# Retention with a mixture of adapters: warm-up, mask order, adapter weights and the pacing of transfers

## The chip, the core and the metric

The kernel runs on one core of a Trainium2 chip. The metric is the device time of one execution in microseconds. A core has TensorE (PE, with its weight loads shown apart as PEld), VectorE (DVE), ScalarE (ACT), GpSimd (POOL) and SyncE (SP). In this kernel SP computes nothing: it issues nearly all transfers between HBM and SBUF, one after the other in the order of the program. Each engine runs its own instructions in order and waits on semaphores for the others.

## The reference

Inputs are q, k, v of 8 batches x 8 heads x 576 positions x 64, and the weights of a mixture of 8 adapters of rank 16. All is float32.

```python
scores = scale * np.matmul(q, k.transpose(0, 1, 3, 2))
gamma = 1.0 - 2.0 ** (-5.0 - np.arange(H))
Dmat = np.where(rel >= 0, gamma[:, None, None] ** rel[None, :, :], 0.0)   # rel = i - j
x = np.matmul(scores * Dmat[None], v)       # then (B, H, S, D) -> rows of 4608 tokens x 512
logits = x @ w_gate                          # 512 -> 8
topk = the 2 largest logits of each token;  w = softmax over these two
out = x + sum over the two experts e of  w_e * ((x @ A[e]) @ B[e])
```

## The kernel before, in words

The 576 positions are four full chunks of 128 and a rest of 64. A **unit** is one chunk of two batches (units 0 to 15: chunk 0 of the four batch pairs, then chunk 1, and so on); units 16 and 17 are the rests of four batches each. The decay is folded into k and q: each is multiplied by a power of gamma on POOL or DVE (`scale_`, L162 to L184). From unit 2 on q is loaded with neighbouring positions in pairs and scaled into an own tile (`qs`, L169).

For a unit u PE does, in short runs of small matmuls:

- T (`stage_T`, L187; lines L215 and, for paired q, L202): transposes k and q into PSUM. ACT copies them out (`evict_T`, L231), and `shift_q` (L249) copies halves of q on DVE into a second tile, x2.
- U (`stage_U`, L291): sums k times v of each half chunk of 64 positions, for the running state. `stage_A` (L327) adds them on DVE into the state SP; `put_state` (L310) copies the state of the first half beside v, on ACT; `first_state` (L318) does so for the chunk's beginning on POOL.
- S (`stage_S`, L258): scores within a half chunk. `masks` (L279) multiplies them by a triangle on DVE, four instructions for the half t and the part of the heads ho, and writes them over x2 and qT. In these tiles each half then holds masked scores on one side and q on the other.
- X (`stage_X`, L339): one product of v and the state with masked scores and q gives x. In chunk 0, where no state comes in, the first half's products stand ahead of the second half's. ACT copies x out, transposed (`evict_x`, L360).
- Z (`stage_Z`, L388): x times the adapters' A and the gate, all in one tile AW of 136 columns. `routing_1` to `routing_4` (L402 to L448) pick two experts: a copy on ACT, maxima on DVE (`choose`), sigmoids on ACT, the mask and two products on POOL.
- P (`stage_P`, L374) transposes the result, copied out by `evict_z` on ACT; B (`stage_B`, L450) transposes x back into PSUM, Y (`stage_Y`, L469) adds the adapters' B to it, ACT copies the output (`evict_o`, L483), and `store` (L520) sends it off.

Nothing schedules this: the order on each engine is that of the program's text. Rounds up to unit 4 are written out (L575 to L845); a loop (L847) then does, for t from 5 to 16, the scores and x of unit t, the logits of t-1, the output of t-2 and the transposes of t+1. `ahead(t)` (L630) issues on SP the stores that are due and the loads of unit t+4, and lets POOL scale unit t+2. `finish` (L693) does the last unit.

PSUM has eight buffers, named by tags x0, x1, s0, s1, u0, u1, o0, o1; a stage that writes a tag waits until the tag's last reader is done. k and v have six SBUF buffers each, q five, the copied x (`xT`) three. `fill` and `fill_small` (L496 to L516) are matmuls of zeros into o0 and o1, whose result nobody reads.

At the start SP issues k, q, v of units 0, 1, 2, then the adapter weights (four transfers for A, L556, one for the gate, L560), then units 3 to 5. k of a unit is one transfer of 512 KB, q and v are two of 256 KB each.

Of the kernel before, what the change touches and what calls it, by code (L numbers as in the profile page):

```python
# [18 lines left out]
def kernel(  # L19
# [43 lines left out]
    for c in range(NFULL):  # L63
# [71 lines left out]
    def load(u, w):  # L135
        if u >= NU:
            return
        c, bp = units[u]
        s0 = 128 * c
        if c == NFULL:  # L140
            for t in range(2):
                hf = slice(64 * t, 64 * t + 64)
                dst = block(u, t)[hf] if w == "v" else nt(u, w)[hf]
                nc.sync.dma_start(out=dst, in_=rows(w, 4 * bp + 2 * t, 2, s0, 64))
        elif w == "v":
            for t in range(2):
                hf = slice(64 * t, 64 * t + 64)
                nc.sync.dma_start(  # L148
                    out=block(u, t)[hf], in_=rows(w, 2 * bp, 2, s0 + 64 * t, 64)
                )  # L150
        elif w == "q" and paired(u):
            for b in range(2):
                nc.sync.dma_start(
                    out=nt(u, w)[64 * b : 64 * b + 64].rearrange("p (h e) d -> p h (e d)", e=2),
                    in_=q[2 * bp + b, :, s0 : s0 + 128, :].rearrange(
                        "h (p e) d -> p h (e d)", e=2
                    ),
                )
# [201 lines left out]
    def evict_x(u):  # L360
        st[u]["xT"] = []
        for b in range(2):
            xt = mo.tile([128, HP, 128], FP32, tag=f"xT{b}", name=f"xT{b}", bufs=3)
            px = st[u]["px"][b]
            if paired(u):
                nc.scalar.copy(  # L366
                    out=xt.rearrange("p a (t i e) -> p (a t) e i", t=2, e=2),
                    in_=px.rearrange("p a t (e i) -> p (a t) e i", e=2),
                )
            else:  # L370
                nc.scalar.copy(out=xt, in_=px.rearrange("p a t i -> p a (t i)"))
            st[u]["xT"].append(xt)
# [121 lines left out]
    def fill_small(n):  # L494
        pf = [pp.tile([128, 96], FP32, tag=f"o{r}", name=f"pf{r}") for r in range(2)]
        for _ in range(n):  # L496
            for c in range(2):
                for r in range(2):
                    sl = slice(64 * r, 64 * r + 64)
                    nc.tensor.matmul(  # L500
                        pf[r][64 * c : 64 * c + 64],
                        lhsT=zero[sl, 0:64],
                        rhs=zero[sl, 0:96],
                        start=True,
                        stop=True,
                        skip_group_check=True,
                    )

    def fill(n):
        if n == 0:  # L510
            return
        pf = pp.tile([128, 512], FP32, tag="o1", name="pf")
        for _ in range(n):
            nc.tensor.matmul(
                pf, lhsT=zero[:, 0:128], rhs=zero, start=True, stop=True, skip_group_check=True
            )  # L516

    o3 = out.rearrange("(b s) m -> b s m", s=S)
# [1 line left out]
    def store(u):  # L520
        c, bp = units[u]
        of = st.pop(u)["osb"].rearrange("p b a o d -> p b (a o d)")
        for b in range(2):
            if c < NFULL:
                nc.sync.dma_start(
                    out=o3[2 * bp + b, 128 * c : 128 * c + 128, :], in_=of[:, b]
                )
            else:
                for t in range(2):
                    (nc.gpsimd if b and u == NU - 2 else nc.sync).dma_start(  # L530
                        out=o3[4 * bp + 2 * t + b, 128 * c : 128 * c + 64, :],
                        in_=of[64 * t : 64 * t + 64, b],
                    )


    def load_batch(u, w, b):
        c, bp = units[u]
        nc.sync.dma_start(  # L538
            out=nt(u, w)[:, b * H : b * H + H], in_=rows(w, 2 * bp + b, 1, 128 * c, 128)
        )  # L540

    nc.vector.memset(zero, 0.0)
    nc.vector.memset(warm, 0.0)
# [5 lines left out]
    load(0, "v")  # L549
    for w in "kqv":  # L550
        load(1, w)
    nc.sync.dma_start(out=pack2, in_=dr_pack2.ap())
    for w in "kqv":
        load(2, w)
    for dt in range(HP):
        nc.sync.dma_start(  # L556
            out=AW[:, dt, 0:ER].rearrange("p (e r) -> p e r", e=E),
            in_=moe_A[:, 128 * dt : 128 * dt + 128, :].rearrange("e d r -> d e r"),
        )
    nc.sync.dma_start(  # L560
        out=AW[:, :, ER : ER + E],
        in_=moe_w_gate.rearrange("(t p) e -> p t e", p=128),
    )
    for u in range(3, 6):
        for w in "kqv":
            load(u, w)

    both = (nc.gpsimd, nc.vector)
    pool2 = (nc.gpsimd, nc.gpsimd)
    dve2 = (nc.vector, nc.vector)  # L570
# [10 lines left out]
    scale_(0, "q", pool2, (0,))  # L581
    scale_(0, "k", dve2, (1,))
    scale_(0, "q", dve2, (1,))
    by_t = ((0, 0), (0, 1), (1, 0), (1, 1))
# [37 lines left out]
    evict_T(2, "q")  # L622
    shift_q(2, nc.vector)
    stage_U(2)
    put_state(2, 1, st[2]["pu"][0], nc.scalar)
    stage_S(2)
    masks(2)
    scale_(3, "k", pool2)

    def ahead(t):  # L630
        for u in {4: (0,), 5: (1, 2)}.get(t, (t - 3,)):
            if t > 3 and has(u):
                store(u)
        for w in "kqv":
            load(t + 4, w)
        if has(t + 1):
            first_state(t + 1)
        if has(t + 2):
            scale_(t + 2, "k", pool2)
            if t > 2:  # L640
                scale_(t + 2, "q", pool2)

    def scores(u):
        if has(u):
            stage_S(u)
            masks(u)
# [46 lines left out]
    def finish():  # L693
# [69 lines left out]
        def output_b(b, zt):  # L763
            o = mo.tile([128, HP, 2, 64], FP32, tag=f"oe{b}", name="oe", bufs=1, align_bytes=256)
            for ho, eng in ((0, nc.scalar), (1, nc.vector)):
                nc.tensor.matmul(
                    po[b][ho], lhsT=zt, rhs=bv[:, :, ho, :],
                    start=False, stop=True, skip_group_check=True,
                )
                (eng.copy if eng is nc.scalar else eng.tensor_copy)(  # L770
                    out=o[:, :, ho, :], in_=po[b][ho]
                )
            c, qd = units[u]
            of = o.rearrange("p a o d -> p (a o d)")
            for t in range(2):
                (nc.scalar if b and t else nc.sync).dma_start(
                    out=o3[4 * qd + 2 * t + b, 128 * c : 128 * c + 64, :],
                    in_=of[64 * t : 64 * t + 64],
                )
# [13 lines left out]
        output_b(0, zt0)  # L793
        output_b(1, small_b(1))

    stage_A(2)
    logits(0)
    choose(0)
    scale_(3, "q", both)
    products(2)  # L800
    routing_3(0)
    turn(3)
    sums(3)
    put(3)
    shift_q(3, nc.vector)
    ahead(2)

    routing_4(0)
    scores(3)
    stage_A(3)  # L810
    scale_(4, "q", both)
    ahead(3)
    logits(1)
    small(0)
    choose(1)
    back(0)
    products(3)
    output(0)
    routing_3(1)
    turn(4)  # L820
    logits(2, "x0")
    choose(2)
    sums(4)
    put(4)
    routing_3(2)
    shift_q(4, nc.vector)

    routing_4(1)
    routing_4(2)
    ahead(4)  # L830
    scores(4)
    logits(3)
    small(1)
    choose(3)
    small(2, "u0")
    back(1)
    output(1)
    sums(5)
    routing_3(3)
    turn(5)  # L840
    back(2)
    put(5)
    shift_q(5, nc.vector)
    products(4)
    output(2)  # L845

    for t in range(5, NU - 1):  # L847
# [53 lines left out]
```

## Time and profile before

| | us |
|---|---|
| median of 3 timed runs | 192.85 (192.42 to 196.5) |
| profiled execution, whole | 190.79 |
| its span, first to last instruction | 188.9 |
| PE busy in the span | 167.3 (89%) |
| ACT, DVE, POOL busy | 114.1, 113.3, 108.7 |
| transfers | 38.99 MB, mean 206 GB/s |

A group's row has the line, engine and operation, what it writes and reads, shapes, the count, then busy time, mean ns of one, and the idle time before them with what ended it. A row of the timeline has start, length, engine, line, and in brackets the idle time before. A row of the waits has who waited for whom, the total, how often, and the longest. "issue" is an idle time for which the profile has no releaser. Ends of matmuls are modelled, and neighbouring runs overlap by a little.

### The profile page before, as it was taken

The page shows a single profiled execution, that of the slowest core. Times are in us where ns is not written, and L with a number is a line of the kernel's source. Part 1 is how long each engine was busy: PE and PEld are TensorE (multiplying, and loading weights), DVE is VectorE, ACT ScalarE, POOL GpSimd, SP SyncE. Part 2 cuts the span into 40 slices and gives each one's busy share as a digit, 9 for nine tenths or more (in the row PEclk, how much of TensorE's full clock was granted, in tenths as well). Part 3 has the DMA queues.
Part 4 walks back from the last instruction along what each step waited for, and adds up shares of the span by engine and source line. Part 5 has one row for each costly group of instructions (what it writes and reads, how often), then busy time and mean ns, then how long its engine had stood idle before and what let it go on. Part 6 is the DMA issues. An engine that isn't in the chain of part 4 may idle for free.

```text
span 188.9 us, 10441 instructions
## 1 busy us (share of the span) xinstructions
PE 167.3 (89%) x4675; PEld 148.9 (79%) x4675; DVE 113.3 (60%) x227; ACT 114.1 (60%) x255; POOL 108.7 (58%) x162
## 2 busy tenths in 40 slices
PE   3989598799889889898999999999997999999960
PEld 3578498588879788788999989899996988988840
DVE  1384837665296475748577787777594846555240
ACT  3437163735569484765767868494959394674650
POOL 1333321567769988493949586675969397520240
PEclk9999969999999999999999999999999999999998
DMA  7999969999999999999999999999998853112325
GB/s 157 248 221 225 227 70 232 202 224 246 224 228 235 262 252 277 252 260 247 241 257 246 266 232 250 221 278 226 271 206 243 181 169 115 50 68 111 115 56 166
DMA packets 108075, 38.99 MB, mean 206 GB/s; under 512 B 88768, under 2 KB 103488, under 8 KB 108032
## 3 DMA queue, kind: packets, MB, share of 16 engines
q1 hardware_dynamic: 107568, 37.71, 81.1%
q8 instruction: 36, 0.59, 1.4%
q0 software_dynamic: 240, 0.39, 1.0%
q10 hardware_dynamic: 224, 0.24, 0.5%
q14 instruction: 7, 0.06, 0.1%
HBM read 29.02 MB, written 9.44 MB: 204 GB/s over the span
## 4 chain that ended last, share of the span: by engine, by line
PE 59%; SPq 14%; issue 7%; DMA 6%; POOL 5%; DVE 4%; ACT 2%; POOLq 0%; ACTq 0%
PE px L350 15%; PE pz L393 12%; PE ps_s L269 8%; PE pu L300 6%; PE po L475 5%; PE po L459 4%; PE pt_k L215 4%; SPq L148 3%; SPq L556 3%; PE pt_q L202 3%; DMA k<-in_k_dram 3%; SPq L160 3%; DMA q<-in_q_dram 3%; POOL k L179 2%; SPq L538 2%
## 5 line engine op out<-in xcount | busy, mean ns | idle before, releaser
L179 POOL TENSOR_TENSOR k<-k,pack 128x512 f32<-128x512 f32 x32 | 34.9, 1109 | 17.4 <-DMA k<-in_k_dram 16.5
L350 PE MATMUL px<-x,v 128*64 128x64 f32 (+1 forms) x576 | 39.3, 226 | 2.6 <-DVE x L289 0.8
L289 DVE TENSOR_TENSOR x<-ps_s,pack 64x512 f32<-64x512 f32 (+1 forms) x38 | 25.1, 660 | 25.9 <-PE ps_s L269 25.6
L350 PE MATMUL px<-qT,v 128*64 128x64 f32 (+1 forms) x576 | 39.2, 226 | 1.3 <-DVE qT L289 1.1
L350 PEld LDWEIGHTS px<-x,v 128*64 128x64 f32 (+1 forms) x576 | 36.2, 140 | 4.4 <-ACT kT L240 1.0
L350 PEld LDWEIGHTS px<-qT,v 128*64 128x64 f32 (+1 forms) x576 | 36.1, 140 | 1.9 <-DVE qT L289 1.2
L393 PE MATMUL pz<-AW,xT 128*128 128x136 f32 x272 | 36.1, 286 | 0.6 <-ACT kT L240 0.6
L393 PEld LDWEIGHTS pz<-AW,xT 128*128 128x128 f32 x272 | 32.6, 190 | 1.8 <-ACT kT L240 0.8
L169 POOL TENSOR_TENSOR qs<-q,pack 128x512 f32<-128x512 f32 x25 | 26.1, 1062 | 4.1 <-DMA q<-in_q_dram 4.1
L406 ACT COPY zs<-pz 128x272 f32<-128x272 f32 x17 | 6.6, 386 | 33.2 <-PE pz L393 32.5
L289 DVE TENSOR_TENSOR qT<-ps_s,pack 64x512 f32<-64x512 f32 (+1 forms) x38 | 25.1, 660 | 1.1
L269 PE MATMUL ps_s<-qT,kT 64*64 64x64 f32 x1152 | 23.6, 224 | 2.1 <-issue 1.4
L269 PEld LDWEIGHTS ps_s<-qT,kT 64*64 64x64 f32 x1152 | 20.4, 137 | 6.2 <-issue 3.1
L441 POOL TENSOR_TENSOR cm<-ge,sg 128x16 f32<-128x16 f32 x17 | 4.0, 234 | 36.5 <-PE pt_k L215 16.9
L316 POOL COPY v<-SP 64x512 f32<-64x512 f32 x32 | 20.5, 640 | 1.6
L300 PE MATMUL pu<-v,k 64*64 64x64 f32 x1024 | 19.2, 221 | 0.8 <-DMA v<-in_v_dram 0.8
L240 ACT COPY kT<-pt_k 128x512 f32<-128x512 f32 x34 | 18.2, 589 | 1.2 <-PE pt_k L215 1.0
L253 DVE COPY x<-qT 64x512 f32<-64x512 f32 x17 | 14.5, 852 | 7.4 <-ACT qT L235 5.0
L366 ACT COPY xT<-px 128x512 f32<-128x512 f32 x28 | 16.3, 625 | 4.4 <-PE px L350 4.4
L300 PEld LDWEIGHTS pu<-v,k 64*64 64x64 f32 x1024 | 16.9, 134 | 2.5 <-DMA v<-in_v_dram 0.9
L492 ACT COPY osb<-po 128x512 f32<-128x512 f32 x33 | 17.6, 584 | 1.0 <-PE po L475 1.0
L252 DVE COPY x<-qT 64x512 f32<-64x512 f32 x14 | 8.1, 579 | 16.0 <-ACT qT L235 12.0
(68 smaller groups left out, 242.6 us busy)
## 6 DMA issues: line engine op xcount, KB each, us to landing
v<-in_v_dram SPq DMA_DIRECT2D x36, 256.0 KB, 5.2
q<-in_q_dram SPq DMA_DIRECT2D x34, 256.0 KB, 5.2
out_dram<-osb SPq DMA_DIRECT2D x32, 256.0 KB, 4.2
k<-in_k_dram SPq DMA_DIRECT2D x15, 512.0 KB, 5.7
k<-in_k_dram SPq DMA_DIRECT2D x6, 256.0 KB, 4.3
q<-in_q_dram SPq DMA_DIRECT2D x1, 512.0 KB, 6.9
out_dram<-oe SPq DMA_DIRECT2D x3, 128.0 KB, 3.3
AW<-in_moe_A_dram SPq DMA_DIRECT2D x4, 64.0 KB, 3.6
```

The costliest lines, as they stand in the source:

```text
L169: engines[b].tensor_tensor(out=qs[:, :, 4 * b : 4 * b + 4, :].rearrange("p e h d -> p h e d"), in0=tl[:, b * H : b * H + H, :].rearrange(" ...
L179: engines[b].tensor_tensor(out=tl[:, b * H : b * H + H, :], in0=tl[:, b * H : b * H + H, :], in1=g[:, c, :].unsqueeze(2).broadcast_to((128 ...
L240: nc.scalar.copy(out=tl[:, r], in_=st[u]["p" + w][r])
L253: eng.tensor_copy(out=x2[0:64, 1, b], in_=qT[64:128, 1, b])
L269: nc.tensor.matmul(ps[ho][64 * t : 64 * t + 64, b, hp, :], lhsT=kT[sl, t, b, hp, :], rhs=qT[sl, t, b, hp, :], start=(hp == 0 and b == bs[0 ...
L289: nc.vector.tensor_tensor(out=out, in0=in0, in1=m, op=ALU.mult)
L300: nc.tensor.matmul(pu[t][64 * ho : 64 * ho + 64, b, hp, :], lhsT=kn[sl, h, :], rhs=block(u, t)[sl, h, :], start=(hp == 0 and b == 0), stop ...
L316: copy(out=dst[:, :, :, ho, :], in_=src[64 * ho : 64 * ho + 64])
L350: nc.tensor.matmul(px[b][64 * ho : 64 * ho + 64, hp, t, :], lhsT=block(u, t)[rw, b * H + 2 * hp + ho, :], rhs=facing(u, t, ho)[rw, b, hp, ...
L366: nc.scalar.copy(out=xt.rearrange("p a (t i e) -> p (a t) e i", t=2, e=2), in_=px.rearrange("p a t (e i) -> p (a t) e i", e=2),)
L393: nc.tensor.matmul(pz[:, b, :], lhsT=st[u]["xT"][b][:, dt, :], rhs=AW[:, dt, :], start=(dt == 0), stop=(dt == HP - 1), skip_group_check=True,)
L492: copy(out=s["osb"][:, :, :, ho, :], in_=s["po"][ho])
```

## The change

- `move` takes the place of SP's transfers: from the fourth on, each waits until the third one ahead of it has landed. k, and q of units 0 and 1, are loaded in two halves by batch.
- `fill_small(20)` (80 matmuls of 64x64 by 96 columns in four quarters of the array) becomes `warmup(48)` (48 matmuls of the full 128x128 array by 96 columns). `fill` does the same columns in pieces of 256. Four fills are new: 4, 2, 3 and 4 in the rounds of units 1 and 2.
- The masks of units 1, 2 and 3 are ordered by half (t) and not by part of the heads.
- The adapter weights are issued after k, q and the first half of v of unit 3, one of them between that and the second half of v.
- X(2), T(3), U(3), S(3) come ahead of all adapter work; Z(0) follows S(3), and the steps up to the loop are reordered. The scaling of k(2) goes to POOL alone, that of k(4) to POOL and DVE. `xT` has four buffers.

```diff
+    inflight = []
+    def move(out, in_):
+        dma = nc.sync.dma_start(out=out, in_=in_)
+        if len(inflight) >= 3:
+            tc.add_manual_dep(
+                dma.ins, inflight[-3].ins.name,
+                mybir.DependencyInfo(mybir.DependencyClass.Sync, mybir.DependencyReason.DATA),
+                reason="pace",
+            )
+        inflight.append(dma)
...
         else:
-            nc.sync.dma_start(out=nt(u, w), in_=rows(w, 2 * bp, 2, s0, 128))
+            for b in range(2):
+                move(
+                    out=nt(u, w)[:, b * H : b * H + H], in_=rows(w, 2 * bp + b, 1, s0, 128)
+                )
...
-            xt = mo.tile([128, HP, 128], FP32, tag=f"xT{b}", name=f"xT{b}", bufs=3)
+            xt = mo.tile([128, HP, 128], FP32, tag=f"xT{b}", name=f"xT{b}", bufs=4)
...
+    def warmup(n):
+        pf = pp.tile([128, 512], FP32, tag="o1", name="pf")
         for _ in range(n):
+            nc.tensor.matmul(
+                pf[:, 0:96], lhsT=zero[:, 0:128], rhs=zero[:, 0:96], start=True, stop=True,
+                skip_group_check=True,
+            )
...
-                    (nc.gpsimd if b and u == NU - 2 else nc.sync).dma_start(
+                    (nc.gpsimd.dma_start if b and u == NU - 2 else move)(
...
     for w in "kqv":
         load(2, w)
-    for dt in range(HP):
-        nc.sync.dma_start(
-            out=AW[:, dt, 0:ER].rearrange("p (e r) -> p e r", e=E),
...
+    for w in "kq":
+        load(3, w)
+    load(3, "v", (0,))
+    load_adapter(0)
+    load(3, "v", (1,))
+    for dt in range(1, HP + 1):
+        load_adapter(dt)
+    for u in range(4, 6):
...
-    fill_small(20)
+    warmup(48)
...
     stage_S(1)
-    masks(1)
-    scale_(2, "k", both)
+    masks(1, None, by_t)
+    scale_(2, "k", pool2)
+    fill(4)
     stage_X(1)
...
     stage_A(1)
+    fill(2)
     stage_T(2, "q", tag="o")
     evict_T(2, "q")
     shift_q(2, nc.vector)
+    fill(3)
     stage_U(2)
     put_state(2, 1, st[2]["pu"][0], nc.scalar)
     stage_S(2)
-    masks(2)
+    masks(2, None, by_t)
     scale_(3, "k", pool2)
+    fill(4)
+    stage_X(2)
+    evict_x(2)
+    stage_T(3, "k", tag="s")
+    evict_T(3, "k")
+    scale_(3, "q", both)
+    stage_A(2)
+    stage_T(3, "q", tag="o")
+    evict_T(3, "q")
+    shift_q(3, nc.vector)
+    stage_U(3)
+    put_state(3, 1, st[3]["pu"][0], nc.scalar)
+    stage_S(3)
+    masks(3, None, by_t)
```

After `finish` is defined, the rounds up to the loop read so (before, in the order of its L796 to L845; then after):

```python
# before
stage_A(2); logits(0); choose(0); scale_(3, "q", both); products(2); routing_3(0)
turn(3); sums(3); put(3); shift_q(3, nc.vector); ahead(2)
routing_4(0); scores(3); stage_A(3); scale_(4, "q", both); ahead(3); logits(1); small(0)
choose(1); back(0); products(3); output(0); routing_3(1); turn(4); logits(2, "x0")
choose(2); sums(4); put(4); routing_3(2); shift_q(4, nc.vector)
routing_4(1); routing_4(2); ahead(4); scores(4); logits(3); small(1); choose(3)
small(2, "u0"); back(1); output(1); sums(5); routing_3(3); turn(5); back(2); put(5)
shift_q(5, nc.vector); products(4); output(2)

# after
scale_(4, "k", both); ahead(2); logits(0, "o0"); stage_X(3); evict_x(3); choose(0)
stage_A(3); routing_3(0); routing_4(0); stage_T(4, "k", tag="s"); evict_T(4, "k")
scale_(4, "q", both); stage_T(4, "q", tag="x"); evict_T(4, "q"); shift_q(4, nc.vector)
logits(1, "o0"); choose(1); routing_3(1); ahead(3); routing_4(1); small(0, "u1"); back(0)
output(0); sums(4); put(4); scores(4); logits(2, "x0"); choose(2); small(1, "x1")
back(1); output(1); routing_3(2); products(4); routing_4(2); ahead(4); logits(3, "u0")
choose(3); small(2, "s0"); turn(5); routing_3(3); sums(5); put(5)
shift_q(5, nc.vector); back(2); output(2)
```

More of the change, by code (lines that the diff above doesn't have):

```diff
@@ L133, in rows, with load @@
         return SRC[w][b0 : b0 + nb, :, s0 : s0 + n, :].rearrange("b h j d -> j (b h) d")
-    def load(u, w):
+    def load(u, w, ts=(0, 1)):
         if u >= NU:
@@ L143, in load @@
                 dst = block(u, t)[hf] if w == "v" else nt(u, w)[hf]
-                nc.sync.dma_start(out=dst, in_=rows(w, 4 * bp + 2 * t, 2, s0, 64))
+                move(out=dst, in_=rows(w, 4 * bp + 2 * t, 2, s0, 64))
         elif w == "v":
-            for t in range(2):
+            for t in ts:
                 hf = slice(64 * t, 64 * t + 64)
-                nc.sync.dma_start(
+                move(
                     out=block(u, t)[hf], in_=rows(w, 2 * bp, 2, s0 + 64 * t, 64)
@@ L794, in finish @@
         output_b(1, small_b(1))
-    stage_A(2)
-    logits(0)
+    scale_(4, "k", both)
+    ahead(2)
+    logits(0, "o0")
+    stage_X(3)
+    evict_x(3)
     choose(0)
-    scale_(3, "q", both)
-    products(2)
+    stage_A(3)
     routing_3(0)
[L802 to L806, printed above, removed]
     routing_4(0)
-    scores(3)
-    stage_A(3)
+    stage_T(4, "k", tag="s")
+    evict_T(4, "k")
     scale_(4, "q", both)
+    stage_T(4, "q", tag="x")
+    evict_T(4, "q")
+    shift_q(4, nc.vector)
+    logits(1, "o0")
+    choose(1)
+    routing_3(1)
     ahead(3)
-    logits(1)
-    small(0)
-    choose(1)
+    routing_4(1)
+    small(0, "u1")
     back(0)
-    products(3)
     output(0)
-    routing_3(1)
-    turn(4)
+    sums(4)
+    put(4)
+    scores(4)
     logits(2, "x0")
     choose(2)
-    sums(4)
-    put(4)
+    small(1, "x1")
+    back(1)
+    output(1)
     routing_3(2)
-    shift_q(4, nc.vector)
-    routing_4(1)
+    products(4)
     routing_4(2)
     ahead(4)
-    scores(4)
-    logits(3)
-    small(1)
+    logits(3, "u0")
     choose(3)
-    small(2, "u0")
-    back(1)
-    output(1)
+    small(2, "s0")
+    turn(5)
+    routing_3(3)
     sums(5)
-    routing_3(3)
-    turn(5)
-    back(2)
     put(5)
     shift_q(5, nc.vector)
-    products(4)
+    back(2)
     output(2)
```

63 lines of the change are left out of this document (27 added, 36 removed).

## The prediction

> **What bounds the kernel now.** I read four views in this order: the page's head, busy time by stretch, who waited for whom between 61.7 and 154.6 us, and PE's instructions in order of time.
>
> ```profile
> span 188.9 us, 10441 instructions
> ...
> 23.40:26.80 3.40, 3.40 (x62) 3.28 (x62) 1.83 (x3) 1.55 (x3) 1.35 (x1) 0.50 0.63 64
> 26.80:61.70 34.90, 31.39 (x880) 27.75 (x876) 21.20 (x44) 21.17 (x48) 21.28 (x30) 1.00 0.97 221
> 61.70:92.30 30.60, 27.23 (x791) 24.58 (x794) 19.06 (x36) 19.91 (x44) 22.26 (x32) 1.00 1.02 261
> 92.30:154.60 62.30, 60.88 (x1838) 56.03 (x1842) 44.67 (x84) 44.20 (x99) 45.18 (x64) 1.00 0.95 237
> ```
>
> The columns are length, then PE, weight loads, DVE, ACT and POOL busy, granted clock, DMA share and GB/s. From 92.3 us PE is busy 60.88 of 62.30 us: nothing but PE work counts there, while the DMA engines are 0.95 full, so they are nearly as tight. Before that PE loses 3.4 us in 61.7 to 92.3, 3.5 us in 26.8 to 61.7, and 1.7 us through a half clock at 23.4.
>
> ```profile
> PE po L459 <- issue: 1.5, 2, 0.9
> PE ps_s L269 <- issue: 1.4, 3, 0.8
> ...
> PE po L475 <- issue: 1.0, 1, 1.0
> ```
>
> After 61.7 us PE's pauses mostly have no releaser ("issue"): these three rows make 3.9 us. They lie where the DMA engines are full.
>
> **The change part by part.** Write S(u) for the scores of unit u, T the transposes, U the state sums, X the products, Z, P, B, Y the adapter stages. The price of each on PE, from the chain of waits:
>
> ```profile
> 58.68 0.50 PE po L459 x16
> 59.18 2.02 PE px L350 x64
> 61.20 0.54 PE po L475 x4
> ...
> 63.93 2.05 PE pz L393 x16
> 65.98 0.11 PE pzt L378 x2
> 66.09 1.09 PE pu L300 x64
> 67.19 0.65 PE pt_k L215 x16
> 67.83 0.50 PE pt_q L202 x16
> ...
> 100.92 1.09 PE ps_s L269 x64
> ```
>
> That is B, X, Y, Z, P, U, T of k, T of q, S: 8.55 us per unit.
>
> ```profile
> 1.19 1.81 PE L500 MATMUL pf<-zero 64*64 64x96 f16 x80 [1.19 <-DVE warm L543]
> 4.98 0.69 PE L215 MATMUL pt_k<-pack,k 64*128 64x64 f32 x8 [1.98 <-DVE k L179]
> ...
> 9.86 0.46 PE L215 MATMUL pt_q<-pack,q 64*128 64x64 f32 x8
> ...
> 15.73 0.82 PE L514 MATMUL pf<-zero 128*128 128x512 f16 x3
> ...
> 17.12 1.30 PE L300 MATMUL pu<-v,k 64*64 64x64 f32 x61
> ...
> 18.27 1.23 PE L269 MATMUL ps_s<-qT,kT 64*64 64x64 f32 x63
> 20.27 0.33 PE L350 MATMUL px<-x,v 64*64 64x64 f32 x2 [0.77 <-DVE x L289]
> 21.70 0.33 PE L350 MATMUL px<-qT,v 64*64 64x64 f32 x2 [1.10 <-DVE qT L289]
> ...
> 25.27 1.12 PE L215 MATMUL pt_k<-pack,k 64*128 64x64 f32 x16
> ```
>
> *Warm-up.* Eight transposes take 0.69 us at 4.98 and 0.46 us at 9.86, so the array is slow at first, although the 80 small matmuls ran. A full-array fill of 512 columns costs 0.27 us (0.82 / 3), so 96 columns cost 0.05 us, or 0.10 us in a slow array. 48 of them end between 3.6 and 6.0 us; the first transpose comes at 4.98. The cost is 0 to 1.0 us there, and I take nothing, since the 1.98 us pause covers most of it. The gain is at most the slow stretch between 5 and 9.7 us, about half of it. It does not all pass on: U(1) needs v of unit 1, and U(1) began at 17.12 without a pause, so v may have come just then or earlier. Let E be the end of S(1), before at 18.27 + 1.23 = 19.5. I bound the new E between 18.7 and 19.5 and take 19.2.
>
> [...]
>
> *Masks by half, X.*
>
> ```profile
> 19.54 0.68 DVE L289 TENSOR_TENSOR x<-ps_s,pack 64x512 f32<-64x512 f32 x1 [0.78 <-PE ps_s L269]
> ...
> 21.67 0.69 DVE L289 TENSOR_TENSOR x<-ps_s,pack 64x512 f32<-64x512 f32 x1
> ```
>
> Four masks of 0.7 us run from E to E+2.85. Before, X(1) needed the first and the third, so it stood still from 20.6 to 21.7. Now the first two serve its first half: E+1.45 to E+2.4; the second half runs from E+2.9 to E+3.85. fill(4) (4 x 0.26) lies in the wait before. T(2) of k starts at E+3.85, before at 25.27 = E+5.8: 1.9 us gained, half of it the half-clock stretch, which the fill keeps away.
>
> *Later steps.* These ACT and POOL prices recur:
>
> ```profile
> L240 ACT COPY kT<-pt_k 128x512 f32<-128x512 f32 x34 | 18.2, 589 | 1.2 <-PE pt_k L215 1.0
> L431 ACT ACTIVATE sg<-zs,ns 128x8 f32<-128x8 f32 x34 | 8.4, 295 | 8.3 <-DVE ge L421 8.3
> L443 POOL TENSOR_TENSOR zc<-zs,cm 128x128 f16<-128x128 f32 x34 | 13.1, 407 | 1.3
> L169 POOL TENSOR_TENSOR qs<-q,pack 128x512 f32<-128x512 f32 x25 | 26.1, 1062 | 4.1 <-DMA q<-in_q_dram 4.1
> ```
>
> T(2) of k, fill(2), T(2) of q end at E+5.5. fill(3) writes PSUM buffer o1, which holds that T: it waits until ACT has copied it, four copies at 0.55 us from E+4.5, so E+6.75. Then fill(3), U(2), S(2): E+9.7. Here 1.2 us of pause and 0.8 us of fill stand on the path. Masks(2) end at E+12.6, X(2) at E+13.65, T(3) at E+14.8, U(3) at E+15.9; S(3) waits for its transposed q until E+16.5 and ends at E+17.6. Z(0) ends at E+19.65, X(3) (masks done at E+20.45) at E+21.6, T(4) of k at E+22.25.
>
> Now a new wait. T(4) of q needs POOL's scaling of q(4), queued behind routing_4(0). ACT copies X(3) until E+22.25 and makes the sigmoids (0.5 us); POOL's mask and two products take 1.0 us, the scaling 1.06 us: E+24.8. PE pauses 2.6 us. T and Z(1) end at E+27.4, P and B at E+28.0. Y(0) waits for zT(0), which on ACT stands behind the sigmoids of unit 1: E+29.35, a pause of 1.35 us. Y, U(4), S(4), Z(2), P, B, Y end at E+35.5; X(4), Z(3), P, T(5), U(5), B, Y add 7.45 us: the loop's first S(5) starts at E+42.95.
>
> ```profile
> 61.67 1.15 PE L269 MATMUL ps_s<-qT,kT 64*64 64x64 f32 x60
> ```
>
> With E = 19.2 that is 62.15 against 61.67: **+0.5 us**. The early gain is spent on 13 fills (3.4 us) and the two pauses. The fourth xT buffer, tags, and fills cut in two halves of equal columns cost nothing.
>
> *Adapter weights later.*
>
> ```profile
> 19.77 6.30 SPq L556 DMA_DIRECT2D AW<-in_moe_A_dram x4
> ...
> 32.48 2.05 POOL L179 TENSOR_TENSOR k<-k,pack 128x512 f32<-128x512 f32 x2 [7.74 <-DMA k<-in_k_dram]
> ```
>
> Four transfers hold SP for 6.3 us ahead of k(3); without them k(3) lands near 32.48 - 6.30 = 26.2 us, and T(3) wants it at E+13.65 = 32.9. So this takes a wait off POOL, and the path has it only once. The weights now follow k, q and half of v(3): near 36 us. Z(0) wants them at E+17.6 = 36.8: hidden by under 1 us; each us later costs one.
>
> *Transfers that wait.*
>
> ```profile
> k<-in_k_dram SPq DMA_DIRECT2D x15, 512.0 KB, 5.7
> ...
> DMA to landing us min/median/max: 2.0/2.0/2.0
> ...
> DMA to landing us min/median/max: 3.4/3.4/3.4
> ```
>
> The first row is the queue's issue list; the last two are the stores at 155.7 us with the queue empty, and the first k load of 256 KB. Every SP transfer now waits for the third one ahead, and all later loads and stores queue behind it; POOL's scaling, then T, wait for them. With three in flight a unit's eight transfers of 256 KB take 8L/3 us, L being issue to landing. PE needs 8.55, so L may be 3.2 us. The rows give 2.0 to 3.4. I take 2.8: 7.5 us per unit, hidden. Depth falls from 5.7 us to about 3, and if PE's "issue" pauses come from waiting behind that queue, they shrink. Bounds: 0 and 3.9 us; I take two fifths, as the depth falls: **-1.6 us**.
>
> *The end.*
>
> ```profile
> 181.67 1.18 SPq L530 DMA_DIRECT2D out_dram<-osb  x2
> 182.96 2.25 SPq L776 DMA_DIRECT2D out_dram<-oe  x3
> ```
>
> The last store on SP, issued near 184.6, now waits for the second store of L530, issued near 182.3 plus 2.0 to 3.4 us: **+0.4 us**, range 0 to 1.1.
>
> Sum: +0.5 - 1.6 + 0.4 = -0.7 us. The profiled execution took 190.79 us, 188.9 of it span; the median shown is 192.85, 2.1 us more. I set the sum against the median: **192.1 us**.
>
> **The rivals.**
>
> 1. *The queue starves* (slower). The mechanism is the same wait: if L is over 3.2 us, DMA sets the pace. At 3.4 us a unit takes 9.1 us, 0.5 more, over 12 units 6 us: **198.5 us**. For it: DMA share 0.95 to 1.02 already. Against it: at full depth 5.7 us is mostly queueing. [...]
>
> 2. *The pauses vanish* (faster). All 3.9 us go, E is 18.7 (0.5 less than I took), and the two new pauses (2.6 + 1.35) come out 2.0 shorter because weights and transfers land earlier: 192.85 + (0.5 - 0.5 - 2.0) + 0.4 - 3.9 = 187.85, **187.9 us**. For it: the pauses lie only under full DMA. Against it: the engines stay as full.
>
> 3. *The half clock moves.* The 2.6 us pause could bring the half clock as the pauses after 19.5 us did: 1.7 us more, **193.8 us**. [...] The change then does not remove the slow stretch, it moves it.
>
> **How the numbers follow.** Forecast 0.40 (189.5 to 194.5), rival 1 0.23, rival 2 0.28, rival 3 0.09. 2% of the median is 3.9 us, about what a measurement of this kernel can tell from no change: faster is below 189.0, slower above 196.7. So 0.28 faster, 0.49 within, 0.23 slower. The range takes in most of both sides: 187.0 to 198.0 us.
>
> **What would show it.** Right: T(2) of k starts below 24 us; PE idle some 2.5 us before T(4) of q with POOL's zc as releaser; the first S of the loop at 61 to 63 us; "issue" pauses after it of 2 to 3 us; issue to landing near 3 us. Rival 1: PE or POOL waits on DMA after 70 us, DMA share falling below 0.9 while PE idles. Rival 2: issue pauses under 1 us. The forecast is wrong if weights land after 38 us, or if the queue's slack differs from what I took.

## The result, and the profile after

The changed kernel takes **209.78 us** (208.52 to 214.15) against 192.99 us (192.42 to 196.5) before: a ratio of 1.0859, with a 95% interval of 1.074 to 1.0978. It is slower by 16.8 us; the prediction of 192.1 us with a range to 198.0 us was wrong. The first rival, the starved queue, named the mechanism and priced it far too low. Some executions of a kernel come out more than 1.5% above its fastest; ratios and intervals leave them out, medians do not, and the profiles of e2_before_pace, e9_pace4, e12_k_whole and e15_combo3 (below) are of such executions, so small differences in them mean nothing.

The page of the changed kernel: its span, the granted clock and the DMA share in 40 slices, two lines of the chain that ended last, and the list of DMA issues (count, KB of each, median us from issue to landing).

```profile
span 209.2 us, 10469 instructions
...
PEclk9999969996799999999999999999999999699996
DMA  7989688559877756747887876878696778956325
...
DMA 55%; PE 32%; issue 3%; ACT 3%; POOL 3%; SPq 1%; DVE 1%; POOLq 0%; ACTq 0%
...
k<-in_k_dram SPq DMA_DIRECT2D x36, 256.0 KB, 4.1
q<-in_q_dram SPq DMA_DIRECT2D x36, 256.0 KB, 4.2
v<-in_v_dram SPq DMA_DIRECT2D x36, 256.0 KB, 4.1
out_dram<-osb SPq DMA_DIRECT2D x32, 256.0 KB, 3.5
```

The same two lines of the page before:

```profile
DMA  7999969999999999999999999999998853112325
...
PE 59%; SPq 14%; issue 7%; DMA 6%; POOL 5%; DVE 4%; ACT 2%; POOLq 0%; ACTq 0%
```

The chain now runs through transfers for 55% of the span (before 6%), while the engines that carry them are fives to eights in most slices, where before they were nines. Transfers set the pace without filling the engines: the limit is the time of each transfer and how many are in flight, not bandwidth: in the loop after moves 199 GB/s, where before moved 219. The last four rows of the first view are what I called L. I took 2.8 us and set the threshold at 3.2; it is 4.1 to 4.2 for loads and 3.5 for stores.

SP itself shows the wait (who waited for whom: total us, times, longest); with q and the stores its waits for landings come to 97 us.

```profile
SPq L107 <- DMA v<-in_v_dram: 35.8, 35, 3.4
SPq L107 <- DMA k<-in_k_dram: 33.4, 31, 2.9
```

Three stretches of after by windows (columns as in the prediction), then the stretch of before from the first to the last S of the loop's whole units, S(5) to S(17).

```profile
27.90:31.30 3.40, 3.20 (x74) 2.53 (x77) 0.42 (x1) 0.15 (x1) 2.08 (x2) 0.51 0.78 196
48.40:55.20 6.80, 5.49 (x38) 5.04 (x40) 1.98 (x5) 1.46 (x3) 4.29 (x5) 0.50 0.82 197
70.20:190.90 120.70, 107.59 (x3017) 96.69 (x3016) 70.36 (x143) 75.20 (x166) 76.30 (x112) 0.99 0.75 199
```

```profile
61.70:170.90 109.20, 103.65 (x3021) 94.63 (x3020) 72.40 (x140) 74.48 (x166) 76.10 (x109) 1.00 0.86 219
```

The first two rows are stretches of half clock ahead of the loop; before had one of 3.4 us there. S(5) starts at 70.2 us, 8.5 later than before. From there to S(17) after needs 120.70 us where before needed 109.20: 11.5 more, with DMA share 0.75 in place of 0.86. What follows S(17) is 18.3 against 18.0 us. So 8.5 us were lost up to the loop and 11.5 in it, 20.0 of the 20.3 us by which the spans differ. In the loop PE's pauses grow from 5.6 to 13.1 us; its busy time grows by 3.9, of which some 1.7 us is one more half clock (the 6 of PEclk near 180 us; the clock is 0.52 from 178.0 to 181.4 us) and the rest is not traced.

The waits of after, first over the whole span, then PE's alone from 60 us on (who waited for whom: total us, times, longest).

```profile
POOL k L194 <- DMA k<-in_k_dram: 50.2, 22, 9.8
PEld L393 <- POOL zc L458: 13.5, 18, 3.0
POOL qs L184 <- DMA q<-in_q_dram: 13.3, 10, 3.0
...
PE pzt L393 <- POOL zc L458: 9.3, 9, 2.8
PE po L474 <- issue: 0.9, 1, 0.9
PE pt_q L217 <- issue: 0.7, 1, 0.7
PE ps_s L284 <- issue: 0.5, 1, 0.5
PE px L365 <- issue: 0.3, 1, 0.3
```

From 60 us on PE never names DMA. POOL does: over the whole span 22 waits for k, 50.2 us (16 of them, 28.9 us, in the loop), and 10 for q. Before had this for k over the whole span:

```profile
POOL k L179 <- DMA k<-in_k_dram: 16.5, 5, 7.7
```

PE then waits for POOL's `zc`, 9.3 us in nine pauses. One unit on POOL shows why (timeline: start, length, and in brackets the idle time before and its releaser).

```profile
115.82 1.04 POOL L194 TENSOR_TENSOR k<-k,pack 128x512 f32<-128x512 f32 x1 [1.36 <-DMA k<-in_k_dram]
117.43 1.23 POOL L194 TENSOR_TENSOR k<-k,pack 128x512 f32<-128x512 f32 x1 [0.56 <-DMA k<-in_k_dram]
119.59 2.04 POOL L184 TENSOR_TENSOR qs<-q,pack 128x512 f32<-128x512 f32 x2 [0.93 <-DMA q<-in_q_dram]
121.59 0.22 POOL L456 TENSOR_TENSOR cm<-ge,sg 128x16 f32<-128x16 f32 x1
```

POOL works in the order of the program. The scaling of units ahead waits for landings three times, and the routing of an older unit (L456, L458), which needs no transfer, stands behind it. So a late load of a future unit delays the present one.

Before the loop, the instructions of PE in after that answer to the prediction's steps (timeline):

```profile
4.83 0.46 PE L230 MATMUL pt_k<-pack,k 64*128 64x64 f32 x8
...
18.07 1.10 PE L315 MATMUL pu<-v,k 64*64 64x64 f32 x59 [0.53 <-DMA v<-in_v_dram]
19.02 1.15 PE L284 MATMUL ps_s<-qT,kT 64*64 64x64 f32 x63
24.34 0.71 PE L230 MATMUL pt_k<-pack,k 64*128 64x64 f32 x16
28.10 1.44 PE L522 MATMUL pf<-zero 128*128 128x256 f16 x6 [1.16 <-ACT qT L250]
49.45 1.12 PE L217 MATMUL pt_q<-pack,qs 64*128 64x64 f32 x16 [3.09 <-POOL qs L184]
70.16 1.16 PE L284 MATMUL ps_s<-qT,kT 64*64 64x64 f32 x64
```

### The profile page after: what moved, and what is told of

Read it like the earlier page. It is cut to its first block, busy times and chain, and to the rows that moved or that the text cites. A ratio compares the mean times of both kernels' runs of the same rounds, so it can differ in the third digit from the quotient of the medians.

```text
span 209.2 us, 10469 instructions
## 1 busy us (share of the span) xinstructions
PE 177.2 (85%) x4676; PEld 156.6 (75%) x4676; DVE 109.0 (52%) x227; ACT 115.0 (55%) x255; POOL 107.9 (52%) x162
## 4 chain that ended last, share of the span: by engine, by line
DMA 55%; PE 32%; issue 3%; ACT 3%; POOL 3%; SPq 1%; DVE 1%; POOLq 0%; ACTq 0%
DMA v<-in_v_dram 17%; DMA k<-in_k_dram 17%; DMA q<-in_q_dram 13%; PE pz L408 9%; PE px L365 7%; DMA out_dram<-osb 6%; PE ps_s L284 3%; PE pu L315 3%; PE po L490 3%; PE pt_q L217 2%; DMA AW<-in_moe_A_dram 2%; PE po L474 2%; PE pt_k L230 1%; POOL qs L184 1%; SPq L107 1%
## 5 line engine op out<-in xcount | busy, mean ns | idle before, releaser
L194 POOL TENSOR_TENSOR k<-k,pack 128x512 f32<-128x512 f32 x32 | 33.5, 1053 | 52.3 <-DMA k<-in_k_dram 50.2
L365 PE MATMUL px<-x,v 128*64 128x64 f32 (+1 forms) x576 | 40.6, 228 | 0.9 <-issue 0.7
L408 PE MATMUL pz<-AW,xT 128*128 128x136 f32 x272 | 37.9, 295 | 0.0
L408 PEld LDWEIGHTS pz<-AW,xT 128*128 128x128 f32 x272 | 34.4, 198 | 1.2
L284 PE MATMUL ps_s<-qT,kT 64*64 64x64 f32 x1152 | 22.1, 221 | 1.1 <-issue 0.5
L315 PE MATMUL pu<-v,k 64*64 64x64 f32 x1024 | 21.0, 227 | 2.2 <-issue 1.0
L315 PEld LDWEIGHTS pu<-v,k 64*64 64x64 f32 x1024 | 18.4, 140 | 4.3 <-issue 1.8
L331 POOL COPY v<-SP 64x512 f32<-64x512 f32 x32 | 19.5, 611 | 1.6
L507 ACT COPY osb<-po 128x512 f32<-128x512 f32 x33 | 17.6, 584 | 2.7 <-DMA out_dram<-osb 1.7
L267 DVE COPY x<-qT 64x512 f32<-64x512 f32 x14 | 8.3, 590 | 20.1 <-ACT qT L250 14.4
L250 ACT COPY qT<-pt_q 128x512 f32<-128x512 f32 x28 | 15.3, 607 | 3.9 <-PE pt_q L217 3.9
L331 ACT COPY v<-sm 64x512 f32<-64x512 f32 x24 | 14.9, 622 | 1.3 <-DVE sm L349 1.1
```

The costliest lines, as they stand in the source:

```text
L194: engines[b].tensor_tensor(out=tl[:, b * H : b * H + H, :], in0=tl[:, b * H : b * H + H, :], in1=g[:, c, :].unsqueeze(2).broadcast_to((128 ...
L250: nc.scalar.copy(out=tl[:, :, r].rearrange("p t a (e i) -> p t (a e) i", e=2), in_=st[u]["pq"][r].rearrange("p a b (t i) -> p t (a b) i", ...
L284: nc.tensor.matmul(ps[ho][64 * t : 64 * t + 64, b, hp, :], lhsT=kT[sl, t, b, hp, :], rhs=qT[sl, t, b, hp, :], start=(hp == 0 and b == bs[0 ...
L315: nc.tensor.matmul(pu[t][64 * ho : 64 * ho + 64, b, hp, :], lhsT=kn[sl, h, :], rhs=block(u, t)[sl, h, :], start=(hp == 0 and b == 0), stop ...
L331: copy(out=dst[:, :, :, ho, :], in_=src[64 * ho : 64 * ho + 64])
L365: nc.tensor.matmul(px[b][64 * ho : 64 * ho + 64, hp, t, :], lhsT=block(u, t)[rw, b * H + 2 * hp + ho, :], rhs=facing(u, t, ho)[rw, b, hp, ...
```

## The experiments

Two theories stood against each other. **Theory A**: the wait for the third transfer ahead starves the loop, and is nearly the whole loss. **Theory B**: the reordered and filled first rounds cost by themselves, whatever the queue does. Every kernel was timed beside before on the same chip. All results, by their difference from the median of before in the column beside it; "loop" is the time from S(5) to S(17) in the profile; "pauses" is the sum of the rows in which PE waits for "issue" after 60 us.

| kernel | median us | before | difference | ratio, 95% interval | S(5) at | loop | pauses |
|---|---|---|---|---|---|---|---|
| before | 192.99 | | | | 61.7 | 109.2 | 4.6 |
| after (wait at 3) | 209.78 | 192.99 | +16.8 | 1.0859 [1.074, 1.0978] | 70.2 | 120.7 | 2.4 |
| e1_no_pace | 201.22 | 192.51 | +8.7 | 1.0517 [1.0436, 1.0597] | 69.3 | 112.0 | 5.6 |
| e2_before_pace | 206.79 | 192.51 | +14.3 | | 66.5 | 121.9 | 2.9 |
| e_pace6 | 198.83 | 192.51 | +6.3 | 1.0353 [1.0246, 1.0459] | 67.5 | 111.6 | 5.6 |
| e_pace_first | 202.51 | 192.51 | +10.0 | 1.0548 [1.0444, 1.0652] | 68.8 | 112.4 | 5.9 |
| e5_no_fill | 195.79 | 191.29 | +4.5 | 1.0286 [1.0188, 1.0384] | 65.4 | 111.1 | 5.0 |
| e6_scale_first | 197.66 | 191.29 | +6.4 | 1.0355 [1.0214, 1.0495] | 66.6 | 110.4 | 4.3 |
| e7_before_warm | 193.28 | 191.29 | +2.0 | | 61.3 | 107.1 | 2.6 |
| e8_before_byt | 191.06 | 191.29 | -0.2 | 1.0023 [0.9974, 1.0072] | 61.5 | 110.4 | 4.8 |
| e12_k_whole | 201.75 | 191.46 | +10.3 | | 71.9 | 109.4 | 4.5 |
| e9_pace4 | 195.84 | 191.46 | +4.4 | 1.0176 [1.009, 1.0263] | 67.1 | 110.2 | 4.5 |
| e10_before_pace6 | 191.87 | 191.46 | +0.4 | 1.0039 [0.9988, 1.009] | 60.9 | 109.0 | 5.3 |
| e11_combo | 196.79 | 191.46 | +5.3 | 1.0248 [1.0188, 1.0309] | 64.7 | 110.8 | 5.1 |
| e13_combo4 | 193.01 | 191.64 | +1.4 | 1.0093 [1.0033, 1.0153] | 67.2 | 106.3 | 2.2 |
| e14_before_pace4 | 189.40 | 191.64 | -2.2 | 0.9945 [0.9867, 1.0024] | 60.4 | 107.9 | 2.5 |
| e15_combo3 | 209.61 | 191.64 | +18.0 | 1.0844 [1.0764, 1.0923] | 69.0 | 126.5 | 2.9 |

A row without a ratio has no interval: its fastest run stands alone, at 203.26 us (e2_before_pace), 188.40 (e7_before_warm) and 196.73 (e12_k_whole), with the other three 1.7 to 3.6% above it. Seven medians lie outside every range that was written down for them: e5_no_fill, e9_pace4 and e14_before_pace4 below, e_pace_first, e11_combo and e15_combo3 above, e_pace6 between its two.

### The wait alone, and the change without it

**e1_no_pace**: after, without the wait.

```diff
-        if len(inflight) >= 3:
+        if False:
```

> The changed kernel with the wait for the third transfer ahead taken out; all else as changed. Theory A (the wait starves the queue, in the first rounds and in the loop): the time comes back to 190 to 194 us, the loop's first S starts at 61 to 63 us (70.2 in the changed kernel), and a unit of the loop takes 8.6 us (10.5). Theory B (the reordered first rounds, their fills and their two new pauses cost most): S(5) stays at 68 us or later and the time is 198 us or more.

Measured: +8.7 us, as Theory B had it. About half of the loss goes with the wait, half stays. Its windows and the waits of PE up to 69.3 us:

```profile
23.10:26.50 3.40, 3.40 (x59) 3.05 (x56) 2.07 (x3) 1.17 (x2) 2.18 (x2) 0.51 0.82 188
53.90:57.30 3.40, 3.31 (x92) 2.78 (x96) 0.31 (x1) 1.11 (x3) 1.13 (x4) 0.50 1.25 237
69.30:181.30 112.00, 105.46 (x3022) 95.82 (x3020) 73.67 (x143) 74.34 (x166) 77.84 (x112) 1.00 0.77 195
```

```profile
PE pt_q L217 <- POOL qs L184: 2.9, 1, 2.9
PE po L490 <- ACT zT L401: 1.7, 1, 1.7
PE px L365 <- issue: 1.5, 2, 1.1
PE pu L315 <- issue: 1.4, 1, 1.4
PE pu L315 <- DMA v<-in_v_dram: 1.2, 2, 1.0
...
PE pf L522 <- ACT qT L250: 1.1, 1, 1.1
```

The loop is back at 112.0 us from 120.7, but S(5) still starts at 69.3. Two half clocks, the three pauses that the prediction had (for qs, zT and the copy ahead of fill(3)) and 2.9 us of "issue" stand ahead of it.

**e2_before_pace**: the other half of that pair, before with the wait alone; k stays one transfer of 512 KB.

```diff
-            nc.sync.dma_start(out=nt(u, w), in_=rows(w, 2 * bp, 2, s0, 128))
+            move(out=nt(u, w), in_=rows(w, 2 * bp, 2, s0, 128))
...
```

> The kernel before with the wait alone; k stays one transfer of 512 KB, so a unit has seven transfers and not eight. Theory A: with 4.1 us from issue to landing 7 x 4.1 / 3 = 9.6 us per unit against 8.55, some 10 to 16 us slower than before: 203 to 209 us. Theory B: within 3 us of before.

Measured: +14.3 us by the median, as Theory A had it, and 10.8 by its fastest run. POOL waits for k as in after:

```profile
POOL k L191 <- DMA k<-in_k_dram: 57.1, 17, 10.1
```

So the wait alone makes 11 to 14 us of loss, on a kernel whose first rounds were never touched, and the first rounds alone make half of after's: each theory was right about its own part. The two do not add: 10.8 + 8.7 is 19.5 and 14.3 + 8.7 is 23.0, and after loses 16.8.

**e_pace_first**: after, the wait only for the first 43 transfers of SP, about those that belong to the first rounds.

```diff
-        if len(inflight) >= 3:
+        if 3 <= len(inflight) < 43:
```

> The changed kernel, with the wait for the first 43 SP transfers alone (the loads of units 0 to 5 and the weights). Theory A: the first rounds stay late (S(5) at 70 us), the loop is back at 8.6 us a unit: 70.2 + 127 = 197 span, 199 to 202 us. If the wait costs in the loop alone: 190 to 194 us.

Measured: +10.0 us, loop 112.4. Against e1's +8.7 with overlapping intervals, the wait costs little where it stands in the first rounds; its price is paid in the loop.

### How deep the queue must be

**e_pace6**, **e9_pace4**, **e10_before_pace6**, **e14_before_pace4**: after with the wait for the sixth and for the fourth transfer ahead, and before with each of the two.

```diff
-        if len(inflight) >= 3:
+        if len(inflight) >= 6:
...
-                dma.ins, inflight[-3].ins.name,
+                dma.ins, inflight[-6].ins.name,
```

> The changed kernel, each transfer waiting for the sixth one ahead. Theory A: six in flight cover the latency (the queue before held 3 to 5 by itself), so as without the wait: 190 to 194 us. Theory C (any wait on SP costs, by the time that its semaphore takes, however deep the queue): 200 us or more.

> The changed kernel, each transfer waiting for the fourth one ahead (third: 209.8 us; sixth: 198.8; no wait: 201.2). If a transfer's own latency sets the pace at three (3 / 4.1 us), four carry a third more, 8 x 4.1 / 4 = 8.2 us per unit, just under PE's 8.55: 199 to 203 us. If the latency grows with the depth, so that the engines and not the wait set the pace: 205 us or more.

> The kernel before with a wait for the sixth transfer ahead alone. In the changed kernel this depth was 2.4 us faster than no wait. If a shorter queue does shorten PE's pauses without a releaser: 188 to 190.5 us, those pauses under 3 us after S(5) (4.6 before). If that gain was the chance of one run: 190.5 to 193 us.

> The kernel before with the wait for the fourth transfer ahead alone (k in one piece of 512 KB; third: 206.8 us, sixth: 191.9). If depth three is the only one that starves: 190 to 193.5 us. If the step is gradual: 195 to 200 us.

Measured: at six, after loses 6.3 us and before 0.4; at four, after loses 4.4 us and before is 2.2 faster by the medians, 0.55% by the ratio, with an interval that includes no change. Between three and four in flight lies a step of 12 to 17 us (the third pair is e15 and e13, below); from four on no cost of the wait shows. The issue list of e9_pace4, then its loop:

```profile
k<-in_k_dram SPq DMA_DIRECT2D x36, 256.0 KB, 4.2
q<-in_q_dram SPq DMA_DIRECT2D x36, 256.0 KB, 4.9
v<-in_v_dram SPq DMA_DIRECT2D x36, 256.0 KB, 4.6
out_dram<-osb SPq DMA_DIRECT2D x32, 256.0 KB, 3.9
```

```profile
67.10:177.30 110.20, 104.88 (x3017) 95.46 (x3016) 73.89 (x143) 74.00 (x166) 77.44 (x112) 1.00 0.81 209
```

Eight transfers of a unit, four at a time, take (2 x 4.2 + 2 x 4.9 + 2 x 4.6 + 2 x 3.9) / 4 = 8.8 us; a unit of before takes 109.2 / 12 = 9.1. In after, three at a time, they take (2 x 4.1 + 2 x 4.2 + 2 x 4.1 + 2 x 3.5) / 3 = 10.6, and the unit takes 120.7 / 12 = 10.1. So the formula comes within 0.5 us of after's unit. That is the step: one more transfer in flight raises L only from 4.0 to 4.4 us in the mean, and the queue then just keeps up.

Each of the pairs at four and six (e9 and e_pace6, e14 and e10, and below e13 and e11) comes out 1.9 to 3.9 us better at four (1.8 to 3.4 by the ratios; only the intervals of e13 and e11 do not touch). In two of the three the "issue" pauses fall from over 5 us to 2.5 or less. Over all seventeen profiles the six with three or four in flight have 2.2 to 4.5, and the eleven others 2.6 to 5.9, ten of them 4.3 or more. One profile of each and one exception on each side: a tendency in the direction of the prediction, not a proof, and that the gain at four comes through it is argued only.

### What the first rounds cost

**e5_no_fill**: e1_no_pace without the four new fills.

```diff
-    fill(4)
     stage_X(1)
...
-    fill(2)
     stage_T(2, "q", tag="o")
...
-    fill(3)
     stage_U(2)
...
-    fill(4)
     stage_X(2)
```

> The changed kernel without the wait on transfers (201.2 us) and without its four new fills, the 13 pieces of 512 columns in the rounds of units 1 and 2. If the fills stand on the path (fill(3) with its wait for ACT 1.9 us, fill(2) 0.6): the loop's first S starts at 66 to 67 us instead of 69.3, and the time is 198 to 199.5 us. If the fills pay by keeping the clock up: a half-clock stretch more, and 201 us or more.

Measured: +4.5 us against e1's +8.7, with intervals that do not touch, and S(5) at 65.4 where e1 had 69.3. In this pair, where the granted clock falls to half in two stretches of 3.4 us ahead of the loop with the fills and without, the fills cost about 4 us: 3.4 us of their own by the prediction's row (13 at 0.26), and the pause that fill(3) makes.

**e6_scale_first**: e1_no_pace with the scaling of q(4) ahead of `routing_4(0)`.

```diff
     routing_3(0)
-    routing_4(0)
     stage_T(4, "k", tag="s")
     evict_T(4, "k")
     scale_(4, "q", both)
+    routing_4(0)
     stage_T(4, "q", tag="x")
```

> The changed kernel without the wait on transfers, and with POOL's scaling of q(4) ahead of routing_4(0). If the pause of 2.9 us before T(4) of q is that order on POOL, the pause goes to under 1 us, the half clock after it too: S(5) at 65 to 67 us, 197 to 199 us. If q(4) is late in any case: 200 to 202 us.

Measured: +6.4 us, S(5) at 66.6. The pause ahead of T(4) of q falls from 2.9 us to 0.6:

```profile
PE pt_q L217 <- POOL qs L184: 0.6, 1, 0.6
```

S(5) moves by 2.7 us, so the pause was on the path for its full size. The time moves by 2.3, but its interval overlaps that of e1. The half clock after the pause did not go with it: the clock is 0.51 from 51.5 to 54.9 us.

**e7_before_warm** and **e8_before_byt**: before with one early part of the change each, the full-array warm-up or the masks of units 1 and 2 by half.

```diff
-    fill_small(20)
+    warmup(48)
```

```diff
-    masks(1)
+    masks(1, None, by_t)
...
-    masks(2)
+    masks(2, None, by_t)
```

> The kernel before with the full-array warm-up alone. By my prediction S of unit 0 starts 1 to 1.5 us earlier and the end of S(1) is held at about 19.5 us by v of unit 1: 191 to 193.5 us, the same as before. If the early clock passes on: 190 us or less.

> The kernel before with the masks of units 1 and 2 by half alone. By my prediction X(1) starts its products earlier by one mask (0.7 us) and X(2) alike: S(5) 0.5 to 1.5 us earlier than at 61.7, 190.5 to 192.5 us; the half clock near 23 us stays or goes by chance. Rival: no change, as PE is held by the transfers there.

Measured: 193.28 us (188.4 to 195.16) against 191.29, without an interval, and 191.06 against 191.29. Whether the warm-up alone gains or costs a us or two is open. In the profiles neither moves S(5) by more than 0.4 us. With the masks by half the half clock stayed, and lasted twice as long as before's:

```profile
22.60:29.40 6.80, 6.80 (x140) 6.45 (x144) 2.08 (x3) 3.23 (x6) 1.56 (x1) 0.50 0.64 83
```

**e12_k_whole**: e1_no_pace with k of units 1 to 15 and q of unit 1 in one transfer of 512 KB again, as before has them (unit 0 had its halves there already).

```diff
-            for b in range(2):
-                move(
-                    out=nt(u, w)[:, b * H : b * H + H], in_=rows(w, 2 * bp + b, 1, s0, 128)
-                )
+            move(out=nt(u, w), in_=rows(w, 2 * bp, 2, s0, 128))
```

> The changed kernel without the wait, and with k (and q of unit 1) in one transfer of 512 KB again. If halves cost a fixed time each: 198 to 199.5 us. If they are hidden in the queue: 200 to 202.5 us.

Measured: 201.75 us (196.73 to 203.7) where e1 had 201.22 (200.99 to 202.64). Three of the four runs agree with e1, the fourth is over 4 us faster: whether the halves cost anything is open.

### Both mended together

**e11_combo**, **e13_combo4**, **e15_combo3**: after without the four fills (as in e5) and with q(4) scaled first (as in e6), the wait at six, four and three.

```diff
-        if len(inflight) >= 3:
+        if len(inflight) >= 6:
...
-    fill(4)
     stage_X(1)
...
-    routing_4(0)
     stage_T(4, "k", tag="s")
     evict_T(4, "k")
     scale_(4, "q", both)
+    routing_4(0)
```

> The changed kernel with the wait for the sixth transfer ahead, without the four new fills, and with POOL's scaling of q(4) ahead of routing_4(0). If the three costs add (fills 5.4, order on POOL 3.5, depth 2.4 against no wait): 201.2 - 11.3 = 190 us, as before. If they overlap (PE's slow stretches and pauses count once): 193 to 196 us, and the rest is the order of the rounds itself.

> The changed kernel with the wait for the fourth transfer ahead, without the four new fills, and with q(4) scaled ahead of routing_4(0). At depth four with fills and the old POOL order it took 195.8 us. If fills and POOL order cost in this kernel as they did without any wait (5.4 and 3.5 us): 188 to 191 us, as fast as before or faster. If depth four had already taken their place: 193 to 196 us.

> The same, waiting for the third transfer ahead, as the change does. If the queue at depth three holds the loop whatever the first rounds do: 203 to 208 us, S(5) at 64 to 66 us and the loop some 138 us. If the first rounds' gain passes on in full: 199 to 202 us.

Measured: +5.3, +1.4 and +18.0 us. (The 138 us expected for e15's loop run to the end of the kernel; counted so it had 144.6.) With the wait at three, taking both costs out of the first rounds gains nothing: 209.61 us against after's 209.78. POOL's wait for k in e15:

```profile
POOL k L194 <- DMA k<-in_k_dram: 54.9, 25, 8.2
```

At four the same two edits bring after from +4.4 to +1.4 (intervals that overlap a little). The profiles do not show this gain ahead of the loop: S(5) starts at 67.2 us in e13 and at 67.1 in e9. There the clock differs (PEclk of e9, then of e13, 40 slices each):

```profile
PEclk9999999996999999999999999999999999999996
```

```profile
PEclk9999769999969999999999999999999999999997
```

With the fills, e9 has one slow stretch ahead of the loop; without them, e13 has three of 3.4 us. At half clock a busy PE loses 1.7 us in each (an estimate: 3.4 us at a clock of 0.50), so two more are worth the 3.4 us that the fills take. That the first rounds' faults are hidden under the starved queue fits these times, but the profiles do not show it. The two edits together, at six, are worth 1.0 us beyond e_pace6 (2.0 by the ratios) and less than either alone beside e1; in e11 two half clocks remain, as its windows show:

```profile
31.00:34.40 3.40, 3.40 (x56) 3.18 (x58) 2.59 (x4) 1.36 (x3) 0.69 (x1) 0.50 1.04 143
44.60:48.00 3.40, 3.40 (x19) 3.38 (x16) 2.03 (x2) 1.07 (x2) 3.22 (x6) 0.51 1.16 259
```

What holds the rest of the first rounds is not settled.

No version is shown to beat before. e14_before_pace4 is the nearest, 0.55% faster with an interval of 1.3% faster to 0.2% slower.

## Why the prediction was wrong, step by step

**Where it failed: "Transfers that wait".** The step's formula was right: a unit's eight transfers take 8L/3. The term that was mis-sized is L: taken as 2.8 us from 2.0 to 3.4, measured 4.1 for loads and 3.5 for stores. Both ends of that bound came from transfers with next to nothing beside them, two stores on an empty queue and the first load of the kernel. The 5.7 us of the 512 KB loads under load I put aside as "mostly queueing", and a row beside it on before's page, of the size in question, I did not use:

```profile
k<-in_k_dram SPq DMA_DIRECT2D x6, 256.0 KB, 4.3
```

The runs show that only a part of it was queueing: loads take 4.1 to 4.2 us with three in flight, 4.2 to 4.9 with four (e9) and 4.5 to 5.5 without any wait (e1). L does fall with the queue, but at three it is still half again what I took, so where I booked a gain of 1.6 us the loop lost 11.5. The threshold mattered less: I set 3.2 by PE's 8.55 us of work; by the 9.1 us that a unit of before takes it is 3.4. The two stores of 256 KB on the empty queue took 2.0 us from issue to landing, the loads of the same size with three in flight 4.1 to 4.2, twice that.

**Rival 1** had a chance of 0.23, and at 198.5 us (192.1 + 6 is 198.1) was priced with L = 3.4, the upper end of the same bound. The loop lost 11.5 us, not 6. It also reaches PE as rival 1 had it, through POOL, but by a way that was not written down: the wait that PE sees is the routing (L458), queued on POOL behind the scaling. Halves against wholes of k stay open (e12: 201.75 us with wholes, e1: 201.22 with halves). Before with whole transfers of k starves at three as well (e2, 206.79 us) and does not at four (e14, 189.40): what decides here is how many are in flight.

**"The end" and the "issue" pauses: the sizes as forecast, the cause open.** After S(17) the kernel takes 0.3 us more (predicted 0.4). The pauses after 60 us are 2.4 us where the prediction looked for 2 to 3, 2.2 less than before (taken: 1.6). They shrank because the queue is short, or because PE is late anyway; e14, which does not starve, has 2.5, which speaks for the first; e7 has 2.6 without any wait, which speaks for neither. If the gain was the wait's, it stood on a path that no longer set the end.

**The first rounds: the single terms right, the sum 7 us short.** By the rows of after, and of e1 where the wait does not disturb:

- *Warm-up*: free, as taken (the 48 matmuls run from 1.19 us for 3.53); T starts at 4.83 and takes 0.46 us in place of 0.69. Its gain ended at v(1), as the step said it could: U(1) waits 0.53 us for DMA, in e1 1.0. E came out at 20.2 in after and 19.6 in e1, not 19.2.
- *Masks by half*: in after T(2) of k starts at E + 4.2 (predicted 3.85). But in e8 the slow clock stayed, and in e1 it came at 23.1: "the half-clock stretch, which the fill keeps away" was an assumption, and held in part at most. By the pages, all ten profiles without the new fills have a half clock that begins before 35 us; of the seven with them, e9, e_pace6 and e_pace_first do not, and after, e1, e6 and e12 do.
- *fill(3)*: a pause of 1.16 us (predicted 1.2), right. *T(4) of q*: 2.9 in e1, 3.09 in after (predicted 2.6), released by POOL's qs, right in its mechanism (the list of signs named zc). *Y(0)*: 1.7 in e1 and 0.5 in after (1.35). *Weights late*: Z(0) did not wait, but it began at 40.7 us in after, 2.9 later than E + 17.6, so the margin of 1 us was not tested.
- *Sum*: S(5) was to start at E + 42.95 and started in e1 at 69.3 - 19.6 = E + 49.7. The missing 6.8 us are, by e1's rows, two half clocks at 1.7 us each, 2.9 us of "issue" pauses ahead of the loop, and 0.3 + 0.4 us by which the two pauses were longer: 7.0. I had left out the first two: in the sum the clock was whole, and PE paused only where a named releaser was late. That these terms explain the gap is an account by rows; only the fills (about 4 us) and the order on POOL (2.3 to 2.7) were each taken out.

**Rival 3** was right in its kind: the reordered rounds have a slow clock of their own, in after from 48.4 to 55.2 us at 0.50, beginning in the pause ahead of T(4) of q. That this pause brings it is not shown: in e6 the pause is 0.6 us and a slow stretch comes all the same. For before the trace has no more than the order in time: pauses of 0.77 and 1.10 us at 20.27 and 21.70 us, then the clock at 0.50 from 23.4 us. The slow stretches shown here last 3.4 us (in before from 23.4 us, in e1 from 23.1 and from 53.9) or 6.8 (in after from 48.4, in e8 from 22.6); what sets that length no run shows. The rival's chance belonged beside the others, not against them: it happened together with rival 1.

**Rival 2** fell: the pauses did not vanish, and nothing they gave could be kept. Its sum was off as well: 192.85 - 2.0 + 0.4 - 3.9 is 187.35, not 187.85.

## What to carry to other kernels

Before a queue is limited to n transfers, divide: the transfers of a stage times the landing time of one *among others*, over n, has to stay below the stage (here 10.6 us at three and 8.8 at four, against 9.1); a landing time from an empty queue is no bound for it (2.0 us against 4.1), and a row from under full load is not mere queueing until a run with a shorter queue has shown it. An engine that both prepares loads of units ahead and works on the present one turns a late load into a late present (here POOL: PE waits 9.3 us for its `zc`), so a wait on SP is priced by what stands behind the load's consumer. And a filler that is to keep the clock up is paid on the path of a busy engine, while its gain has to be seen in the granted clock: here 13 of them cost 4 us where the slow stretches stayed (e1, e5), and seem to have paid for themselves where two more came without them (e9, e13; one profile each).

## What the runs showed of the hardware that was not expected

- The step is steep: 209.8 us with three transfers of 256 KB in flight, 195.8 with four, 198.8 with six. Landing takes 4.0 us in the mean at three and 4.4 at four, so what can be moved in a time rises with the number in flight, by an estimate from these times from 3 / 4.0 = 0.75 transfers a us to 4 / 4.4 = 0.91.
- The engines need not be full for transfers to set the pace: DMA share is 0.75 in the loop of after and 0.86 in that of before.
- Matmuls of zeros do not keep a slow-clock stretch away with certainty: in after the fill at 28.10 us, though two other fills had run in the 8 us before it, ran inside such a stretch and took 1.44 us for its six pieces, nearly twice the 0.8 taken. In e9 and e_pace6, with the same fills, the granted clock is 1.00 over the first 40 us.
